# The last six of nine token blocks of a second feed-forward layer: plain blocks replaced by Strassen pairs

## Chip, cores and metric

The kernel runs on one core of a Trainium2 chip. The metric is the device time of one execution in microseconds (us); lower is better. Engines are named as in the profile: PE is TensorE's matmul side and PEld its weight load, DVE is VectorE, ACT is ScalarE, POOL is GpSimd, SP is SyncE, which here only issues DMAs.

## What is computed

A chunked attention is followed by two feed-forward layers over 4608 tokens with model width 512 and hidden width 2048. Only the second layer is touched by the change.

```python
def _moe2_ref(x, w_in, w_out, s, b):      # x 4608x512, w_in 512x2048, w_out 2048x512
    h = x @ w_in
    r = np.maximum(h, 0.0)
    g = s * (r * r) + b
    return (g @ w_out).astype(np.float32)
```

## The kernel before

The 4608 tokens are cut into `NB` = 9 blocks of `TB` = 512. A layer is 9 x 16 = 144 steps, one for each block and each of the `MF` = 16 tiles of 128 hidden columns; steps 0 to 143 are the first layer and 144 to 287 the second. Activations and weights are kept as two parts, hi and lo (`xh`, `xl`, and the pairs of `w_in` and `w_out`), and a product is three matmuls: hi by hi, hi by lo, lo by hi. So a step has 24 matmuls, each with a 128x128 weight tile and 512 columns: `mm1` (L451 to L453) does 4 tiles of the contraction x 3, and `mm2` (L469) does 4 output tiles x 3, two steps behind (`LAG`). All 32 pairs of weight tiles of a layer stay in SBUF (`wp`, tags `w0_0` to `w1_15`).

Between the two, each step of the second layer takes the hidden tile out of PSUM on ACT with Relu, Square and an affine Identity (`ew_a`, L576 to L578), and DVE makes its hi and lo parts (`ew_hi` L614, `ew_lo` L618). The hidden tile has three PSUM banks in turn (`h_bank`), and the output of a block has four (`acc0`, `acc1`), which `evac` empties once in 16 steps. `x2_load` fetches the next block from DRAM scratch (`x2d`), and `store` sends rows of 512 floats to the output. The first two blocks of a layer are run in two halves, since their weights are still being prepared.

Every engine runs its instructions in the order in which they stand. Up to step 33 that order is a table (`START`), from 128 to 165 another (`TURN`); elsewhere it is the loop over `i`, and from step 166 on that loop does the rest of the second layer. SP issues nearly all DMAs, in order, and no more than eight of them are open at a time: each waits for the landing of the one that had its semaphore before. `mm2_last` does the last two steps of `mm2` output tile by output tile, with a store after each.

## Time and profile before

| | |
|---|---|
| device time, median of 3 runs | 1712.54 us (1711.9 to 1712.77) |
| span of the profiled execution, first to last instruction | 1710.9 us |
| PE busy | 1662.3 us, 97% |
| DVE busy | 1026.4 us, 60% |
| ACT busy | 979.8 us, 57% |
| POOL busy | 675.2 us, 39% |
| DMA traffic | 100.24 MB, mean 59 GB/s |

The page gives the span and not the execution's own device time; the median of the runs is 1.6 us above the span. Busy shares are means over stages that differ: in the last third of the span, where the second layer's plain steps run, DVE and ACT are far less busy than in the first two. A matmul's record is longer than the pace at which matmuls follow each other, since they are pipelined, so the pace is read from how many start in a stretch.

### The profile page before, as it was taken

How to read it: one execution, taken by the hardware profiler on the slowest of the kernel's cores; microseconds unless marked ns; L12 is line 12 of the kernel's file. 1: busy time of each engine (PE TensorE's matmuls, PEld its weight loads, DVE VectorE, ACT ScalarE, POOL GpSimd, SP SyncE). 2: the span in 40 equal slices, each digit the busy share in tenths (PEclk: the TensorE clock that was granted, in tenths of full speed). 3: DMA queues.
4: the chain of work that ended last, by engine and by line, in shares of the span. 5: the costliest groups of instructions: out<-in, count | busy, mean ns of one | idle time of the engine just before them, and what ended most of it. 6: DMA issues, size and time to landing. Idle time of an engine off the chain costs nothing.

```text
span 1710.9 us, 25404 instructions
## 1 busy us (share of the span) xinstructions
PE 1662.3 (97%) x9424; PEld 1365.1 (80%) x9424; DVE 1026.4 (60%) x1652; ACT 979.8 (57%) x1590; POOL 675.2 (39%) x576
## 2 busy tenths in 40 slices
PE   4789999999999999999999999999999999999998
PEld 3568777888888888888888888888888888888887
DVE  5899998887887878887799675322222222222222
ACT  5877765666666666666777776443444443434433
POOL 4678865655655656666667553000000000000000
PEclk8799999999999999999999999999999999999999
DMA  9634224222122222121312342101010000101010
GB/s 216 152 109 116 75 58 98 38 59 35 31 58 38 63 35 55 33 60 32 124 52 97 117 151 86 37 16 30 21 25 25 22 28 15 36 8 43 0 25 25
DMA packets 220859, 100.24 MB, mean 59 GB/s; under 512 B 182336, under 2 KB 198720, under 8 KB 220736
## 3 DMA queue, kind: packets, MB, share of 16 engines
q1 hardware_dynamic: 215344, 94.69, 22.0%
q10 hardware_dynamic: 5392, 3.93, 0.9%
q8 instruction: 74, 1.21, 0.3%
q14 instruction: 49, 0.40, 0.1%
HBM read 75.50 MB, written 23.07 MB: 58 GB/s over the span
## 4 chain that ended last, share of the span: by engine, by line
PE 89%; DVE 5%; ACT 2%; DMA 2%; issue 1%; SPq 1%; POOL 1%; ACTq 0%; DVEq 0%; POOLq 0%
PE acc L469 42%; PE h L451 15%; PE h L453 14%; PE h L452 14%; PE pat L343 1%; PE pat L318 1%; PE pat L282 1%; DMA wst<-in_moe_w_in_dram 1%; DVE h L603 1%; DVE t L604 1%; DVE ah L602 1%; DVE w L396 0%; DVE t L585 0%; POOL w L399 0%; DMA vs<-in_v_dram 0%
## 5 line engine op out<-in xcount | busy, mean ns | idle before, releaser
L451 PE MATMUL h<-xh,w 128*128 128x512 f32 x1152 | 457.0, 397 | 10.2 <-DVE t L604 6.2
L453 PE MATMUL h<-xh,w 128*128 128x512 f32 x1152 | 450.0, 391 | 0.0
L452 PE MATMUL h<-xl,w 128*128 128x512 f32 x1152 | 449.7, 390 | 0.0
L576 ACT ACTIVATE r<-h 128x512 f32<-128x512 f32 x144 | 85.9, 596 | 382.4 <-PE h L453 372.1
L469 PE MATMUL acc<-gh,w 128*128 128x512 f32 x1152 | 285.5, 390 | 0.6 <-ACT gh L612 0.6
L469 PE MATMUL acc<-w,gh 128*128 128x512 f32 x1136 | 280.5, 389 | 0.0
L614 DVE CAST gh<-r 128x512 fp32r<-128x512 f32 x134 | 60.9, 455 | 339.3 <-ACT r L578 326.6
L451 PEld LDWEIGHTS h<-xh,w 128*128 128x128 f32 x1152 | 216.9, 188 | 59.0 <-DVE t L604 8.3
L453 PEld LDWEIGHTS h<-xh,w 128*128 128x128 f32 x1152 | 216.9, 188 | 46.3
L469 PEld LDWEIGHTS acc<-gh,w 128*128 128x128 f32 x1152 | 215.6, 188 | 46.0 <-ACT gh L612 1.0
L452 PEld LDWEIGHTS h<-xl,w 128*128 128x128 f32 x1152 | 217.2, 189 | 43.9 <-DVE xl L359 0.5
L469 PEld LDWEIGHTS acc<-w,gh 128*128 128x128 f32 x1136 | 213.2, 188 | 44.3
L564 POOL TENSOR_SCALAR r<-ah,ab_sb 128x512 f32<-128x512 f32 x138 | 111.0, 805 | 234.3 <-ACT ah L547 234.1
L567 POOL TENSOR_TENSOR r<-r,ah 128x512 f32<-128x512 f32 x140 | 182.7, 1305 | 13.7 <-ACT r L562 2.2
L618 POOL TENSOR_TENSOR gl<-t,gh 128x512 fp32r<-128x512 f32 x129 | 168.1, 1304 | 16.1 <-ACT gh L612 14.2
L469 PE MATMUL acc<-gl,w 128*128 128x512 f32 x576 | 154.1, 389 | 0.0
L469 PE MATMUL acc<-w,gl 128*128 128x512 f32 x568 | 151.8, 389 | 0.0
L602 DVE SCALAR_TENSOR_TENSOR ah<-r,h 128x512 f32<-128x512 f32 x144 | 98.3, 682 | 78.5 <-ACT h L595 78.5
L612 ACT ACTIVATE gh<-t 128x512 fp32r<-128x512 f32 x144 | 90.9, 631 | 77.0 <-DVE t L604 71.0
L469 PEld LDWEIGHTS acc<-gl,w 128*128 128x128 f32 x576 | 108.0, 188 | 22.6 <-POOL gl L618 0.3
L399 POOL TENSOR_TENSOR w<-w,wst 128x512 int32<-128x512 int32 x64 | 93.9, 1477 | 78.0 <-DVE w L396 47.8
L469 PEld LDWEIGHTS acc<-w,gl 128*128 128x128 f32 x568 | 106.6, 188 | 22.2
(92 smaller groups left out, 2147.4 us busy)
## 6 DMA issues: line engine op xcount, KB each, us to landing
wst<-in_moe_w_out_dram SPq DMA_DIRECT2D x30, 512.0 KB, 4.6
wst<-in_moe_w_in_dram SPq DMA_DIRECT2D x29, 512.0 KB, 5.0
x2d<-o SPq DMA_DIRECT2D x52, 256.0 KB, 2.7
...
out_dram<-o SPq DMA_DIRECT2D x68, 128.0 KB, 2.4
...
```

The costliest lines, as they stand in the source:

```text
L399: eng.tensor_tensor(out=w, in0=w, in1=st[:, :, 0], op=ALU.add)
L451: T.matmul(h, wh, xh[:, kk], start=kk == 0, stop=False)
L452: T.matmul(h, wh, xl[:, kk], start=False, stop=False)
L453: T.matmul(h, wl, xh[:, kk], start=False, stop=kk == KD - 1)
L469: T.matmul(o, l, r, start=first and n == 0, stop=last and n == 2)
L564: eng.tensor_scalar(out=r, in0=ah, scalar1=ab_sb[:, 1:2], scalar2=ab_sb[:, 0:1], op0=ALU.mult, op1=ALU.add)
L567: eng.tensor_tensor(out=r, in0=r, in1=ah, op=ALU.mult)
L576: A.activation(r, h_t[i], AF.Relu)
L602: V.scalar_tensor_tensor(out=t, in0=r, scalar=ONE, in1=y, op0=ALU.add, op1=ALU.mult)
L612: A.activation(gh, tmp[i]["g"], AF.Copy)
L614: V.tensor_copy(gh, tmp[i]["g"])
L618: (eng or (G if i < N1 else V)).tensor_tensor(out=gl, in0=tmp.pop(i)["g"], in1=f(g_t[i][0]), op=ALU.subtract)
```

## The change

The program is the same, instruction by instruction, up to the start of step 166 on every engine. From there a new function, `finish`, replaces the loop. Steps 166 to 191, which end the two halved blocks and block 2, stay plain. The remaining six blocks become three pairs, and each pair of blocks is multiplied by Strassen's scheme in the variant with 15 sums, in both matmuls of the layer: 7 products of quarter size in place of 8.

- **Weights.** During the plain steps `conv` runs 16 times. Each run joins hi and lo of two weight tiles (`whole`), makes four sums (`tt`), splits them again (`hi` on ACT, `lo` on DVE), and writes the seven operands to DRAM scratch `wq_d` (`as_is`, `put`). In the pairs, `wi_load` and `wo_load` bring them back, 512 KB a time, 84 and 84 in all.
- **Input of a pair.** `x_load` fetches its two blocks from `x2d`; DVE makes four sums of 128x1024 (`x_part`), ACT and DVE split seven operands (`x_hi`, `x_lo`).
- **First matmul of a pair.** It has 8 sets of 7 products (`m1`), each of 6 matmuls. Four hidden tiles of a set come from three chains of PSUM banks: `chain` copies a partial sum out of bank A on ACT before PE goes on adding to it, and `h_sum` adds the other bank's part on DVE.
- **Between.** `g_relu` and `g_square` on ACT, four sums (`mix`) on DVE, and seven splits (`g_hi` on ACT, `g_lo` on DVE). Scale and bias move behind the second matmul: the column sums of `w_out` (`csum_add` on POOL, `bias_mm`) give the bias.
- **Second matmul.** It has 14 half products (`m2`) for every two sets, each of 6 matmuls, so 56 a pair. Each is added into `acc` in SBUF (`out_add`, 48 a pair on DVE and 8 on ACT); eight `out_affine` on ACT bring the bias in.
- **Output.** It comes out transposed; `leave` turns it in 32x32 squares on DVE and `leave_out` writes it with 64 DMAs a pair, each of 32 KB in runs of 32 floats. In the last pair, ACT issues half of them.
- **Order.** `Plan` lists all these steps with costs, dependencies and counts of free tiles, and sorts them by a greedy list schedule (`order`). PE's own order is fixed by hand: in the pairs one product of the first matmul alternates with one half product of the second, 14 places behind; the last 14 half products of the last pair stand alone. `m1_op` and `m2_op` hold what each waits for.

```diff
-X2 = (41,) + tuple(range(52, 140, 16))
+ORDER = (1, 2, 6, 5, 7, 4, 3)
...
+    wq_d = {(k, u): dram.tile([P, 14, 2, 2 * P], F32, name=f"wq{k}_{u}") for k in range(2) for u in range(HF // 2)}
...
-    def mm2_last():
...
+        def add(self, name, eng, cost, fn, *args, after=(), take=None, give=(), lat=0.1, early=None, two=False, kb=0):
...
+            now = {n: max(0.0, o["due"] - o["early"]) if o["early"] is not None else 0.0 for n, o in ops.items()}
...
+                    key = (s, o["due"])
+                    if best is None or e == best[3] and (s < best[0] - 0.05 or abs(s - best[0]) <= 0.05 and o["due"] < best[1]) or e != best[3] and key < best[:2]:
+                        best = (s, o["due"], n, e)
...
+    def finish():
+        i0, i1 = TURNED, N1 + 3 * MF
+        plan = Plan()
+        op = plan.add
+        MM = 0.2267
+        PRE = i1 - 5
...
+            def whole(x):
+                if x == 0:
+                    load()
+                h = f(w_tiles[kind, s + HF * x])
+                V.tensor_tensor(out=st["w"][:, x], in0=h[:, 0], in1=h[:, 1], op=ALU.add)
+
+            def as_is(k, x, y):
+                SP.dma_start(out=at(k), in_=f(w_tiles[kind, s + HF * x])[:, :, y * 2 * P:(y + 1) * 2 * P])
...
+            def tt(o, i, j, how):
+                V.tensor_tensor(out=cut(*o), in0=cut(*i), in1=cut(*j), op=how)
...
+            def hi(x):
+                st[x] = spare.tile([P, 2, 2, 2 * P], F32R, "wo")
+                A.activation(st[x][0][:, :, 0], st["w"][:, x].rearrange("p (n c) -> p n c", n=2), AF.Copy)
+
+            def lo(x, eng):
+                o = st[x][0]
+                eng.tensor_tensor(out=o[:, :, 1], in0=st["w"][:, x].rearrange("p (n c) -> p n c", n=2), in1=f(o[:, :, 0]), op=ALU.subtract)
+
+            def put(x, ks):
+                for y, k in enumerate(ks):
+                    SP.dma_start(out=at(k), in_=f(st[x][0][:, y]))
...
+            op(p + "s1", "V", 0.44, tt, a22, a21, a22, ALU.add, after=[p + "w1"], two=True)
+            op(p + "s3", "V", 0.44, tt, a21, a11, a21, ALU.subtract, after=[p + "s1"], two=True)
+            op(p + "s2", "V", 0.44, tt, a11, a22, a11, ALU.subtract, after=[p + "s3"], two=True)
+            op(p + "s4", "V", 0.44, tt, a12, a12, a11, ALU.subtract, after=[p + "s2"], two=True)
+            if kind:
+                op(p + "cs", "G", 1.4, csum_add, after=[p + "s4"])
...
+        def bias_mm():
+            o = ps["bias"] = ps_a.tile([P, TB], F32, tag="att", name="pb")
+            for z in range(KD):
+                for x in (0, 2) if z < 2 else (0,):
+                    T.matmul(o[:, z:z + 1], csum[:, (z + x) * P:(z + x + 1) * P], ones, start=x == 0, stop=x == 2 or z >= 2)
...
+        def x_load(t):
...
+            xx[t] = {0: r0[:, 0:2], 1: r0[:, 2:4], 3: r1[:, 0:2], 5: r0[:, 2:4], 6: r1[:, 2:4]}
+            for y in range(2):
+                SP.dma_start(out=hold["raw"][y], in_=x2d[PAIRS[t][y]].rearrange("k p c -> p k c"))
...
+        def x_part(t, what):
+            r0, r1 = hold["raw"]
+            b11, b21, b12, b22 = r0[:, 0:2], r0[:, 2:4], r1[:, 0:2], r1[:, 2:4]
+            if what == "T3":
+                xx[t][4], xx[t, 4] = main.tile([P, 2, N], F32, "t3")
+                V.tensor_tensor(out=xx[t][4], in0=b22, in1=b12, op=ALU.subtract)
+            elif what == "T1":
+                V.tensor_tensor(out=b12, in0=b12, in1=b11, op=ALU.subtract)
+            elif what == "T2":
+                xx[t][2], xx[t, 2] = main.tile([P, 2, N], F32, "t2")
+                V.tensor_tensor(out=xx[t][2], in0=xx[t][4], in1=b11, op=ALU.add)
+            else:
+                V.tensor_tensor(out=b21, in0=b21, in1=xx[t][2], op=ALU.subtract)
...
+        def x_hi(t, k):
+            xs[t, k] = main.tile([P, 2, N], F32R, "xs"), main.tile([P, 2, N], F32R, "xs")
+            A.activation(xs[t, k][0][0], xx[t][k], AF.Copy)
+
+        def x_lo(t, k, eng):
+            (hi, _), (lo, _) = xs[t, k]
+            eng.tensor_tensor(out=lo, in0=xx[t][k], in1=f(hi), op=ALU.subtract)
...
+        def wo_load(y):
+            wo[y] = main.tile([P, 2, 2, 2 * P], F32R, "wo2")
+            u, z = divmod(y % (7 * NG), 7)
+            SP.dma_start(out=f(wo[y][0]), in_=wq_d[1, u][:, 2 * z:2 * z + 2])
...
+        def m1(t, s, k):
+            p = ORDER[k]
+            b = "C" if p == 2 else "E" if p in (5, 3) else "A"
...
+            q = 7 * (NSETS * t + s) + k
+            w, tag = wi[q // 2]
+            w = w[:, q % 2]
+            (hi, _), (lo, _) = xs[t, k]
+            terms = [(z, 0, hi) for z in range(2)] + [(z, 1, hi) for z in range(2)] + [(z, 0, lo) for z in range(2)]
+            for n, (z, l, x) in enumerate(terms):
+                T.matmul(ps[b], w[:, l, z * P:(z + 1) * P], x[:, z], start=n == 0 and p in (1, 2, 5), stop=n == 5, skip_group_check=True)
...
+        def chain(t, s, c):
+            A.activation(g_new(t, s, c), ps["A"], AF.Copy)
+
+        def h_sum(t, s, c):
+            g = gt[t, s, c]
+            V.tensor_tensor(out=g, in0=ps["C" if c == "11" else "E"], in1=g, op=ALU.add)
+
+        def g_relu(t, s, c):
+            if c == "21":
+                A.activation(g_new(t, s, c), ps["A"], AF.Relu)
+            else:
+                A.activation(gt[t, s, c], gt[t, s, c], AF.Relu)
...
+        def g_square(t, s, c):
+            A.activation(gt[t, s, c], gt[t, s, c], AF.Square)
...
+        def mix(t, s, c):
+            o, i, j, how = {
+                "22": ("22", "22", "12", ALU.subtract), "12": ("12", "12", "11", ALU.subtract),
+                "11": ("11", "22", "11", ALU.add), "21": ("21", "21", "11", ALU.subtract),
+            }[c]
+            V.tensor_tensor(out=gt[t, s, o], in0=gt[t, s, i], in1=gt[t, s, j], op=how)
...
+        def g_hi(t, s, c, k):
+            gx[t, s, k] = main.tile([P, 2, N], F32R, "gs")
+            A.activation(gx[t, s, k][0][:, 0], gt[t, s, c], AF.Copy)
+
+        def g_lo(t, s, c, k):
+            g = gx[t, s, k][0]
+            V.tensor_tensor(out=g[:, 1], in0=gt[t, s, c], in1=f(g[:, 0]), op=ALU.subtract)
...
+        def m2(t, u, j):
...
+            if p == 2:
+                pool, tag = (ps_a, "att") if dp else (ps_h, "h2")
+                ps["c2", dp] = pool.tile([P, TB], F32, tag=tag, name="hc2")
...
+            for n, (e, l, g) in enumerate(terms):
+                T.matmul(
+                    o, w[:, e, l, dp * P:(dp + 1) * P], gx[t, 2 * u + e, k][0][:, g],
+                    start=n == 0 and p in (1, 2, 5), stop=n == 5, skip_group_check=True,
+                )
+            if dp:
...
+        def out_add(t, u, k, dp):
+            if "acc" not in hold:
+                hold["acc"] = [xp.tile([P, KD, N], F32, tag=tag, name="acc") for tag in ("xh", "xl")]
+            y, z = where[ORDER[k]]
+            o, i = hold["acc"][y][:, z + dp], bank2(k, dp)
+            if u == 0 and ORDER[k] in (1, 6, 5, 4):
+                A.activation(o, i, AF.Copy)
+            elif u == NG - 1:
+                V.scalar_tensor_tensor(out=o, in0=i, scalar=s_sb, in1=o, op0=ALU.mult, op1=ALU.add)
+            else:
+                V.tensor_tensor(out=o, in0=i, in1=o, op=ALU.add)
...
+        def leave(t, y, z):
+            lt[t, y, z] = small.tile([P, N], F32, "ot")
+            V.transpose(lt[t, y, z][0], hold["acc"][y][:, z])
+
+        def leave_out(t, y, z, h, both):
+            o, tag = lt[t, y, z]
+            s0 = PAIRS[t][y] * CH
+            rows = out.rearrange("(b s) d -> s b d", b=B)
+            for x in range(4):
+                (A if both else SP).dma_start(
+                    out=rows[s0 + 32 * h:s0 + 32 * h + 32, :, z * P + 32 * x:z * P + 32 * x + 32],
+                    in_=o[32 * x:32 * x + 32].rearrange("p (b h i) -> p b h i", b=B, h=2)[:, :, h],
+                )
...
+            b4 = f"{t},{s - 1}" if s else f"{t - 1},{NSETS - 1}"
+            c = f"{t},{s}"
+            wait = {
+                0: [f"r21{b4}"] if t or s else [f"Kr{PRE - 1}", f"Kr{PRE - 2}", f"Kr{PRE - 3}"], 1: [f"hs11{b4}", "biasout" if s or t else None], 2: [f"c11{c}"], 3: [f"hs12{b4}"],
+                4: [f"c12{c}"], 5: [f"c22{c}"], 6: [f"hs22{c}"],
+            }[k]
...
+            if last and k in (1, 4, 5, 6):
+                op(f"lv{t},{y},{z}", "V", 0.72, leave, t, y, z, after=[f"o{k}{c},{dp}"], take=("s", 1))
+                for h in range(2):
+                    act = h == 1 and t == NPR - 1
+                    op(f"lo{t},{y},{z},{h}", "A" if act else "S", 2.4, leave_out, t, y, z, h, act, after=[f"lv{t},{y},{z}", f"lo{t},{y},{z},0" if h else None], lat=2.5, kb=128, give=[("s", 1)] if h else ())
...
+                op(f"wi{q // 2}", "S", 0.55, wi_load, q // 2, after=[made[0, s_, k_] for s_, k_ in kk], take=("m", 1), lat=2.5, kb=512, early=AHEAD)
...
+        AHEAD, HOLD = 9.0, 16.0
+        for i in range(i0, i1):
...
+        for z in range(14 - slot):
+            l1(slot)
+            slot += 1
+        for z in range(len(every)):
+            if slot < len(every):
+                l1(slot)
+                slot += 1
+            l2(z)
+        order = plan.order({"m": 0, "s": 4, "c": 6})
+        for n in order:
+            o = plan.ops[n]
+            o["fn"](*o["args"])
+        return plan
 
     with tc.manual_schedule():
...
-            for j, at in enumerate(X2, 2):
-                if e == at:
-                    x2_load(j)
-                if 2 <= e - at < 2 + KD:
-                    x2_hi(j, e - at - 2)
-                    x2_lo(j, e - at - 2)
-        mm2_last()
+            if i % N1 in (3 * HF - 1, 4 * HF - 1):
+                part_load(steps[i][0])
+
+        wq.extend(due(1))
```

**In the plain steps and inside a pair**, PE's row of work looked like this (`acc`: output banks; `h`: hidden bank; `w_0` to `w_15`: weight tiles):

```order
L469 MATMUL acc_14133<-w_13_10844,gh 128x512 x2
L469 MATMUL acc_14134<-w_13_10844,gh 128x512 x2
L469 MATMUL acc_14133<-w_13_10844,gl 128x512 x2
L469 MATMUL acc_14134<-w_13_10844,gl 128x512 x2
L451 MATMUL h<-xh,w_0_9142 128x512
L452 MATMUL h<-xl,w_0_9142 128x512
L453 MATMUL h<-xh,w_0_9142 128x512
```

and now, inside the first pair (`ae`, `hc_`: output banks; `hA`, `hc`, `hE`: hidden banks; `wi`, `wo`: loaded weight operands), it is:

```order
L1033 MATMUL ae_12395<-gs,wo_12282 128x512 x6
L972 MATMUL hc<-xs,wi 128x512 x6
L1033 MATMUL ae_12396<-gs,wo_12282 128x512 x6
L972 MATMUL hA<-xs,wi 128x512 x6
L1033 MATMUL hc_12448<-gs,wo_12334 128x512 x6
L972 MATMUL hE<-xs,wi 128x512 x6
L1033 MATMUL hc_12478<-gs,wo_12334 128x512 x6
```

Twelve matmuls of one kind in a row have become six, and every six go to a bank whose earlier content another engine has to take first. On ACT, at the same place, before (`r`: hidden tile):

```order
L576 ACTIVATE r_14883<-h_14870 128x512
L577 ACTIVATE r_14883<-r_14883 128x512
L578 ACTIVATE r_14883<-r_14883,b2_sb_95,s_sb_94 128x512
L576 ACTIVATE r_14916<-h_14903 128x512
L577 ACTIVATE r_14916<-r_14916 128x512
L578 ACTIVATE r_14916<-r_14916,b2_sb_95,s_sb_94 128x512
```

and now (`g11` to `g22`: the four hidden tiles of a set; `gs`: operands of the second matmul):

```order
L983 ACTIVATE g12_12767<-hA_12701 128x512
L996 ACTIVATE g11_12717<-g11_12717 128x512
L1007 ACTIVATE gs_12792<-g21_12528 128x512
L1007 ACTIVATE gs_12794<-g21_12671 128x512
L983 ACTIVATE g22_12810<-hA_12701 128x512
L993 ACTIVATE g22_12810<-g22_12810 128x512
L996 ACTIVATE g22_12810<-g22_12810 128x512
```

Two copies out of bank `hA_12701` stand four places apart; PE may add to the bank again only behind each of them, with one half product of the second matmul between the second copy's source and its next use.

**Where one pair passes to the next**, SP had, before (`o`: output tiles):

```order
L487 DMA out_0_dram<-o_13540 64x512 x4
L487 DMA out_0_dram<-o_13543 64x512 x4
L424 DMA xl_13656<-x2d7_88 128x512 x4
L487 DMA out_0_dram<-o_14098 64x512 x4
L487 DMA out_0_dram<-o_14101 64x512 x4
L424 DMA xl_14214<-x2d8_89 128x512 x4
L487 DMA out_0_dram<-o_14656 64x512 x4
L487 DMA out_0_dram<-o_14659 64x512 x4
```

and now (`ot`: turned output tiles; `wi`, `wo2`: weight operands):

```order
L1071 DMA out_0_dram<-ot_13563 32x8x32 x4
L949 DMA wi_13592<-wq0_1_91 128x1024
L954 DMA wo2_13602<-wq1_0_94 128x1024
L1071 DMA out_0_dram<-ot_13600 32x8x32 x4
L1071 DMA out_0_dram<-ot_13563 32x8x32 x4
L949 DMA wi_13654<-wq0_1_91 128x1024
L954 DMA wo2_13658<-wq1_0_94 128x1024
L1071 DMA out_0_dram<-ot_13600 32x8x32 x4
L1071 DMA out_0_dram<-ot_13639 32x8x32 x4
L949 DMA wi_13711<-wq0_1_91 128x1024
L954 DMA wo2_13723<-wq1_0_94 128x1024
```

Eight stores of 32 KB now stand between one pair of weight loads and the next. DVE, at the same place, had before:

```order
L618 TENSOR_TENSOR gl_14642<-r_14603,gh_14640 128x512
L525 COPY o_14659<-acc1_14134 128x512 x2
L614 CAST gh_14679<-r_14636 128x512
L618 TENSOR_TENSOR gl_14681<-r_14636,gh_14679 128x512
L614 CAST gh_14722<-r_14675 128x512
```

and now:

```order
L1011 TENSOR_TENSOR gs_13519<-g11_13356,gs_13519 128x512
L1052 SCALAR_TENSOR_TENSOR acc_12420<-ae0_12395,s_sb_102,acc_12420 128x512
L1052 SCALAR_TENSOR_TENSOR acc_12419<-hc2_13395,s_sb_102,acc_12419 128x512
L1064 STREAM_TRANSPOSE ot_13563<-acc_12419 128x512
L1011 TENSOR_TENSOR gs_13555<-g11_13517,gs_13555 128x512
L1052 SCALAR_TENSOR_TENSOR acc_12420<-ae1_12396,s_sb_102,acc_12420 128x512
L1011 TENSOR_TENSOR gs_13567<-g21_13471,gs_13567 128x512
L1011 TENSOR_TENSOR gs_13582<-g22_13447,gs_13582 128x512
L1064 STREAM_TRANSPOSE ot_13600<-acc_12419 128x512
L1052 SCALAR_TENSOR_TENSOR acc_12419<-ae0_12395,s_sb_102,acc_12419 128x512
```

Output additions (L1052), turns (L1064) and splits (L1011) share DVE's row.

## Rows read from the trace of the kernel before

**Rows 1.** The page: span, busy time by engine, and the span in 40 slices.
```profile
span 1710.9 us, 25404 instructions
...
PE 1662.3 (97%) x9424; PEld 1365.1 (80%) x9424; DVE 1026.4 (60%) x1652; ACT 979.8 (57%) x1590; POOL 675.2 (39%) x576
...
PE   4789999999999999999999999999999999999998
...
PEclk8799999999999999999999999999999999999999
```

**Rows 2.** Windows: busy us (x instructions) of PE, PEld, DVE, ACT, POOL, clock, DMA.
```profile
1041.50:1705.50 664.00, 664.00 (x2931) 549.55 (x2929) 172.83 (x299) 274.44 (x414) 9.01 (x7) 1.00 0.10 26
```

**Rows 3.** Waits from 1100 to 1650 us: total, times, longest.
```profile
ACT r L576 <- PE h L453: 314.9, 101, 3.3
```

**Rows 4.** Timeline at 1300 us: start, duration, engine, line.
```profile
1300.01 0.39 PE L453 MATMUL h<-xh,w 128*128 128x512 f32 x1
...
1300.44 0.60 ACT L576 ACTIVATE r<-h 128x512 f32<-128x512 f32 x1 [3.33 <-PE h L453]
...
1303.10 0.69 DVE L432 TENSOR_TENSOR xl<-xl,xh 128x512 fp32r<-128x512 f32 x1 [4.69 <-ACT xh L428]
...
1303.71 0.42 DVE L614 CAST gh<-r 128x512 fp32r<-128x512 f32 x1
```

**Rows 5.** Groups by shape, DVE and ACT, 1100 to 1650 us: total, mean ns.
```profile
L618 DVE TENSOR_TENSOR gl<-r,gh 128x512 fp32r<-128x512 f32 x101 | 70.9, 702 | 13.5 <-PE acc L469 2.7 <-DVE gh L614 0.5
...
L578 ACT ACTIVATE r<-r,b_sb,s_sb 128x512 f32<-128x512 f32 x102 | 83.2, 816 | 3.4
L577 ACT ACTIVATE r<-r 128x512 f32<-128x512 f32 x102 | 64.5, 632 | 3.3
L576 ACT ACTIVATE r<-h 128x512 f32<-128x512 f32 x101 | 60.4, 598 | 314.9 <-PE h L453 314.9
```

**Rows 6.** The same over the whole span: DVE, ACT, PE.
```profile
L586 DVE SCALAR_TENSOR_TENSOR t<-t,a_sb,h 128x512 f32<-128x512 f32 x144 | 107.7, 748 | 5.1
...
L585 DVE TENSOR_TENSOR t<-t,h 128x512 f32<-128x512 f32 x144 | 97.0, 673 | 9.6 <-ACT ah L547 4.7 <-ACT t L553 3.4
...
L270 DVE STREAM_TRANSPOSE qkT<-qk 128x512 f32<-128x512 f32 x56 | 36.4, 687 | 0.1
...
L523 ACT ACTIVATE o<-acc 128x1024 f32<-128x1024 f32 x10 | 10.2, 1022 | 0.4 <-PE acc L469 0.3
...
L259 PE MATMUL pat<-ident,qk 128*128 128x128 f32 x52 | 12.0, 399 | 18.3 <-DMA qk<-in_q_dram 11.7 <-issue 3.9 <-ACT eT L328 2.4
```

**Rows 7.** Timeline of SP's issues: start, duration, line, count.
```profile
301.51 3.79 SPq L216 DMA_DIRECT2D qk<-in_q_dram  x8
305.35 4.75 SPq L216 DMA_DIRECT2D qk<-in_k_dram  x8
...
981.76 0.50 SPq L376 DMA_DIRECT2D wst<-in_moe_w_out_dram  x1
```

**Rows 8.** The page, DMA issues: count, KB each, us to landing.
```profile
wst<-in_moe_w_out_dram SPq DMA_DIRECT2D x30, 512.0 KB, 4.6
...
out_dram<-o SPq DMA_DIRECT2D x68, 128.0 KB, 2.4
```

**Rows 9.** Windows: the last two numbers are DMA share and GB/s.
```profile
301.00:307.00 6.00, 6.00 (x86) 4.85 (x85) 5.83 (x11) 2.77 (x6) 3.47 (x4) 1.00 0.32 50
307.00:313.00 6.00, 6.00 (x28) 4.95 (x28) 4.66 (x10) 4.52 (x8) 3.29 (x4) 1.00 0.36 63
...
980.00:990.00 10.00, 10.00 (x46) 8.29 (x45) 4.11 (x5) 8.47 (x14) 4.41 (x4) 1.00 0.88 301
```

**Rows 10.** Timeline at the end of the span.
```profile
1705.38 0.40 PE L499 MATMUL acc<-w,gl 128*128 128x512 f32 x1
...
1706.55 0.42 DVE L503 COPY o<-acc 128x256 f32<-128x256 f32 x1 [0.99 <-ACT o L502]
1707.00 0.50 ACTq L487 DMA_DIRECT2D out_dram<-o  x1
```

More of the change, by code (lines that the diff above doesn't have):

```diff
@@ L236, in tile_chunk_attention__then__rational_ffn__then__relu2_ffn, with big @@
     turn = itertools.count()
+    bigs = itertools.cycle(range(4))
+    def big(shape, dtype, name):
+        return ap_.tile(shape, dtype, tag=f"big{next(bigs)}", name=name, bufs=1)
     begun = -1
@@ L447, in mm1 @@
         ph = 0 if jj < NB else 1
-        h = h_bank(i)
+        h = h_bank(i) if bank is None else bank
         for kk in range(KD):
@@ L751, in tile_chunk_attention__then__rational_ffn__then__relu2_ffn @@
         play(START)
[L753 to L760 removed]
+        for i in range(BEGUN, TURN_AT):
+            mm1(i)
             att_out(2 * i - 1, 0)
```

437 lines of the change are left out of this document (396 added, 41 removed).

## Prediction

> **What bounds the kernel now.** I read the page first, then a window over the stretch that the change replaces, then who waits for whom in it. The page has PE busy for 97% of 1710.9 us, with all slices but the first three and the last at 9 and a clock granted in full from the third on [rows 1]. From 1041.5 to 1705.5 us, which is step 166 to the end, PE is busy for 664.00 of 664.00 us, and 2931 matmuls start [rows 2]; the program has 122 steps x 24 = 2928 there. One matmul therefore takes 664.00 / 2931 = 0.2265 us, and a plain step 5.44 us. ACT waits for PE 101 times, 314.9 us in all [rows 3], while no wait of PE in this stretch shows: PE is the bound. What takes matmuls off PE shortens the span, as long as the others keep up with the new pattern. The question is what they do then.
>
> **What is removed.** A pair has 2 x 16 steps x 24 = 768 matmuls now, and 8 x 7 x 6 + 56 x 6 = 672 afterwards. Three pairs save 288 x 0.2265 = **65.2 us**. A pair then takes 152.2 us of PE, and one of its eight sets 19.03 us. Of the work added there PE itself has only `bias_mm`: six matmuls of one column and a wait for column sums. The nearest row is a 128x128 transpose of 0.399 us [rows 6], so 6 x 0.4 = 2.4 us at most if nothing waits, and I take **2 us** (0 to 4).
>
> **DVE in the pairs.** Per set: 3 `h_sum` with an operand in PSUM at 0.673 [rows 6], 4 `mix` and 7 `g_lo` at 0.702 [rows 5], 9.74 us. Per pair: 48 `out_add`, 34 at 0.673 and 14 with a scale at 0.748 [rows 6], 33.4 us; 11 of 128x1024, taken as two of 0.702, 15.4 us; 8 turns at 0.687 [rows 6], 5.5 us. Together 8 x 9.74 + 54.3 = 132.2 us of 152.2, 87%. It is not even. By the order, between one `h_sum` of tile 11 and the next, DVE has 18.5, 18.5, 19.1 and 19.1 us in the four sets around the passage from pair to pair, against 19.03 us of PE. Durations overstate DVE: an operation of 0.69 us started at 1303.10 and the next, independent one at 1303.71, 0.61 later [rows 4]. With 25 operations a set that gives back up to 2 us. So DVE keeps pace but has nothing to spare in eight sets. I charge these 0 to 1.5 us each and take 0.4, **3 us**.
>
> **ACT in the pairs.** Per set 4 reads of PSUM at 0.598 and 14 operations at 0.632 [rows 5], 11.2 us; per pair 8 more reads, 8 affine at 0.816 [rows 5] and 7 of 128x1024 at 1.022 [rows 6], 18.5 us. Sum 108.4 of 152.2 us, 71%. The load is not the danger, the latency is. The second copy out of bank A (`c22`) must be over before the next-but-one group of PE, and only one half product lies between, 6 x 0.2265 = 1.36 us. The row: the last matmul of a step starts at 1300.01, ACT at 1300.44 [rows 4], that is 0.2 us after PE's slot of 0.23 is over; then 0.60 us of copy and about 0.1 back. 0.9 of 1.36 us, so 0.4 us are left, less than one ACT operation. If ACT has just begun a split (0.63) PE waits some 0.2 us. 24 sets at 0 to 0.5 us; I take 0.12, **3 us**.
>
> **Loads of weights.** 168 loads of 512 KB in 24 sets are 3.67 MB per 19.03 us, 193 GB/s. The trace has 301 GB/s at a share of 0.88 for 10 us [rows 9], so 342 at full share, and the loads want 56%. A load lands after some 4.6 us [rows 8], and the planner may start it 9 us ahead of its due time; away from a passage they cost nothing. If this cover fails, PE stands.
>
> **The passage from pair to pair.** Here lie the 64 stores of 32 KB. In the first passage SP has 64 stores and 18 loads in a row, which feed 36 groups of PE, 36 x 1.36 = 48.9 us. The nearest row to such a store is the load of q and k, with the same 32x8x32 shape: 8 in 3.79 us and the next 8 in 4.75 [rows 7], 0.54 us each from start to start; a load of weights takes 0.50 [rows 7]. 64 x 0.54 + 18 x 0.50 = 43.6 us. SP is nearly full but not over. The DMA engines: in 12 us, 20 issues of such short runs took a share of 0.32 and 0.36 [rows 9], 4.1 us of all engines, 0.2 each; 64 make 13 us, 18 loads at 342 GB/s 27.6, sum 41 of 48.9 us. Every weight load stands behind eight stores, so what a store takes more than this falls on PE. Two passages at 0 to 12 us; I take 2 each, **4 us**, since both sums stay under 48.9.
>
> No row of before shows a write to DRAM in runs under 512 bytes. The Trainium skill, DMA: Bandwidth & Descriptors, section Specifications, says that below 512 B a DMA engine does a read-modify-write. No run here shows it; by that rule a store here would cost more than the q load that I took, and the time would be that of the second rival below, some 1689 us in place of 1667.
>
> **Plain steps 166 to 191.** 26 x 5.44 = 141 us. Sixteen `conv` bring DVE 16 x (4 x 0.70 + 4 x about 0.40) = 70 us beside some 45 of its own and the first input; 7 DMAs of 256 KB each make 1.8 MB per 8 us. Both fit. I take **1 us** (0 to 4).
>
> **The end.** Now the last matmul is over at 1705.78 and the span at 1710.9, 5.1 us with half a copy, an issue of 0.50 and a store [rows 10]. Afterwards the last 14 half products run alone, at 1.36 us each, and each goes to a bank that DVE must empty one group earlier: 0.2 + 0.75 us and a turn in between are close to 1.36, **1.5 us** (0 to 4). Six outputs are turned in the last six groups. SP has 24 stores for them, and ACT 24 more beside it. The first is ready 5 x 1.36 before PE's end plus 0.2 + 0.75 + 0.69, 5.2 us before; 24 x 0.54 = 13.0 us bring SP to 7.8 us after PE's end, and a store lands 2.4 us later [rows 8]: 10.2, which is **5 us** more than now (3 at 0.47 an issue; 9 where stores land late).
>
> **Sum.** 65.2 - 2 - 3 - 3 - 4 - 1 - 1.5 - 5 = 45.7 us. The span would be 1665.2 us. The page does not give the execution's own time, and the median of the runs is 1.6 us above the span, so I forecast 1666.8, **1667 us**. With every cost at its low end (3 us for the end alone) it would be 1650; with those of this case at their middle to upper ends 1677.
>
> **Rivals.**
> 1. *Nothing waits.* Bias 1, end 3, nothing else: 1712.5 - 61 = 1652 us. For it: DVE's overlap [rows 4] and its low charge per operation. Against it: nine tenths of DVE and of SP in the same 50 us.
> 2. *The stores hold up the loads.* If a short write takes twice the engines' time of the short read, a passage needs 26 + 27.6 = 54 us of 48.9; if it lands so late that eight open DMAs bind, say 6 us, an issue takes 0.75 and the passage 82 x 0.75 = 61.5. That is 5 to 12.6 us a passage in place of 2, and 24 x 0.75 instead of 13 at the end, 5 more, with late landing up to 8: 1667 + 6 to 21 + 5 to 8, about 1689 us. For it: no row shows such a write. Against it: 0.2 us for the read.
> 3. *In-order rows feed each other's lateness.* DVE late by 1.5 us in the eight full sets and ACT's copy by 0.5 in all 24 make 12 + 12 in place of 6: 1685 us. For it: 0.4 us of slack behind `c22`. Against it: the overlap.
> 4. *The weight stream is the bound (slower).* Weights that lay in SBUF now come from DRAM, 88.1 MB in 3 x 152.2 = 456.7 us. The saving is gone when this takes 457 + 46 us, at 175 GB/s. At 144 GB/s it is 612 us and the kernel takes 1667 + 155 = 1822 us. Against it: 301 GB/s over 10 us, though on reads of another shape [rows 9].
>
> **Chances.** Forecast 0.55, rival 1 0.08, rival 2 0.20, rival 3 0.14, rival 4 0.03. The range leaves out rival 4, the better half of rival 1 and the worse half of rival 2: 1653 to 1694 us. 0.2% (3.4 us) is about what can be told from no change; all cases but rival 4 are faster by far more. Faster 0.96, same 0.01, slower 0.03.
>
> **What would show it.** In the profile afterwards PE starts 288 - 6 matmuls fewer, and inside a pair a window of 19 us has 84 of them at full clock. Idle time ahead of `m1` and `m2` should be under 1 us a set, put down to ACT (bank A) and DVE. At the passages SP's row should show stores about 0.54 us apart; a PE that waits for `wi` or `wo2` there speaks for rival 2, idle time spread over all sets for rival 3, and waits for weights away from the passages for rival 4. DVE near 87% and ACT near 71% inside a pair test the counts. The forecast is wrong if the end takes over 14 us or a passage over 4.

## The result and the profile after

The changed kernel takes 1671.19 us (median of four, 1670.4 to 1672.47) against 1712.46 us before: ratio 0.976, 95% interval 0.9747 to 0.9774. The forecast was 1667.0, its range 1653 to 1694. The profiled execution took 1671.37 us for a span of 1669.6, so the span fell by 41.3 us [rows 1], where 65.2 us of matmuls left PE. Where the other 23.9 us went is the question of what follows.

The page of the changed kernel, busy time, and two lines of the 40 slices:

```profile
PE 1607.8 (96%) x9148; PEld 1315.7 (79%) x9148; DVE 1310.4 (78%) x2063; ACT 1092.1 (65%) x1824; POOL 690.1 (41%) x584
...
PE   4799999999999999999999999899999999999997
...
PEclk8899999999999999999999999899999999999999
```

PE starts 276 matmuls fewer: 288 less, and 12 rows for the six of the bias. Before, every slice between the third and the last was at 9 [rows 1]; now one slice in the twenties is not, in PE and in its clock: the 26th, some 1044 to 1085 us. That is the stretch of plain steps with the weight sums beside them, not the pairs. The windows say the same (PE busy and matmuls, granted clock, DMA share, GB/s; a window counts every matmul that overlaps it). The first line is of the kernel before, the others of the changed one:

```profile
1041.50:1080.00 38.50, 38.50 (x172) 1.00 0.29 83
...
1041.50:1080.00 38.50, 32.29 (x122) 0.87 0.88 290
...
1065.00:1070.00 5.00, 0.93 (x3) 0.85 1.03 364
1070.00:1075.00 5.00, 5.00 (x12) 0.50 1.00 349
```

The first window holds 122 matmuls where it held 172; at 0.2265 us each that is some 11 us lost. A busy PE is not a working PE: from 1070 to 1075 us it is busy all the time with 12 matmuls, where 5 us at full clock start 22, since its clock was granted at 0.50, the level of 1.2 GHz, after 4 us of waiting. All waits of PE from 1041 us to the end (total, times, longest):

```profile
PE acc L478 <- DVE o L523: 4.1, 1, 4.1
PE acc L478 <- ACT gh L610: 2.1, 1, 2.1
PE ae L1033 <- DVE acc L1054: 1.2, 2, 0.6
PE ae L1033 <- DVE acc L1052: 0.7, 1, 0.7
PE hA L972 <- ACT g L983: 0.7, 1, 0.7
PE ae L1033 <- ACT gs L1007: 0.3, 1, 0.3
```

No weight load is among them. The first two are the plain steps, and the timeline of the four engines shows how each came about (start, duration, engine, line, count, and the idle time before with what ended it):

```profile
1045.41 0.63 ACT L413 ACTIVATE w<-w 128x512 fp32r<-128x512 f32 x1 [4.66 <-POOL w L406]
1045.94 0.61 ACT L610 ACTIVATE gh<-r 128x512 fp32r<-128x512 f32 x1
...
1046.61 2.57 PE L478 MATMUL acc<-w,gh 128*128 128x512 f32 x8 [2.08 <-ACT gh L610]
...
1062.70 5.76 DVE L441 TENSOR_TENSOR xl<-xl,xh 128x512 fp32r<-128x512 f32 x4
1068.39 1.27 DVE L523 COPY o<-acc 128x512 f32<-128x512 f32 x2
...
1064.45 3.46 POOL L530 TENSOR_TENSOR o<-o 128x512 f32<-128x512 f32 x2 [0.50 <-ACT o L521]
...
1069.72 2.93 PE L478 MATMUL acc<-w,gh 128*128 128x512 f32 x6 [4.07 <-DVE o L523]
```

First hole: the rounding of step 165's hidden tile (L610) went from DVE to ACT, where it stands behind the last weight's rounding (L413), which waits 4.66 us for POOL. Second hole: the eviction of the first half's sums (`evac`, L523) stands on DVE behind four `x2_lo` (L441), which take 1.44 us each and not 0.7, while POOL adds beside them; PE has nowhere to put the next block's sums. PE's restart is slow as well: six matmuls in 2.93 us, where full clock takes 1.5.

The passage from pair to pair and the end:

```profile
1387.87 5.63 SPq L1071 DMA_DIRECT2D out_dram<-ot  x8
...
1648.45 11.21 PE L1033 MATMUL ae<-gs,wo 128*128 128x512 f32 x48 [0.70 <-DVE acc L1052]
...
1649.04 17.51 SPq L1071 DMA_DIRECT2D out_dram<-ot  x32
```

SP has stores and loads in one row from 1358 to 1406 us, and PE waits for none of them. The last matmul is over at 1659.7, the span 9.9 us later.

### The profile page after: what moved, and what is told of

Same layout as the page of the kernel before. It is cut to its first block, busy times and chain, and to the rows that moved or that the text cites. A ratio compares the mean times of both kernels' runs of the same rounds, so it can differ in the third digit from the quotient of the medians.

```text
span 1669.6 us, 26182 instructions
## 1 busy us (share of the span) xinstructions
PE 1607.8 (96%) x9148; PEld 1315.7 (79%) x9148; DVE 1310.4 (78%) x2063; ACT 1092.1 (65%) x1824; POOL 690.1 (41%) x584
## 4 chain that ended last, share of the span: by engine, by line
PE 83%; DVE 10%; issue 2%; ACT 2%; POOL 2%; DMA 1%; SPq 0%; DVEq 0%; ACTq 0%; POOLq 0%
PE acc L478 26%; PE ae L1033 12%; PE h L460 9%; PE h L462 9%; PE h L461 9%; PE hA L972 8%; PE hE L972 4%; PE hc L972 2%; PE hc L1033 2%; PE pat L350 1%; DVE h L601 1%; PE pat L325 1%; PE pat L289 1%; DVE t L602 1%; DVE ah L600 1%
## 5 line engine op out<-in xcount | busy, mean ns | idle before, releaser
L460 PE MATMUL h<-xh,w 128*128 128x512 f32 x768 | 308.4, 402 | 9.0 <-DVE t L602 5.0
L461 PE MATMUL h<-xl,w 128*128 128x512 f32 x768 | 301.4, 392 | 0.3 <-DVE xl L366 0.3
L462 PE MATMUL h<-xh,w 128*128 128x512 f32 x768 | 301.3, 392 | 0.0
L1033 PE MATMUL ae<-gs,wo 128*128 128x512 f32 x864 | 219.6, 391 | 2.3 <-DVE acc L1054 1.2
L1033 PEld LDWEIGHTS ae<-gs,wo 128*128 128x128 f32 x864 | 161.7, 188 | 38.8 <-DVE acc L1054 2.4
L460 PEld LDWEIGHTS h<-xh,w 128*128 128x128 f32 x768 | 145.5, 189 | 43.1 <-DVE t L602 8.3
L616 POOL TENSOR_TENSOR gl<-t,gh 128x512 fp32r<-128x512 f32 x129 | 167.7, 1301 | 16.1 <-ACT gh L610 14.4
L462 PEld LDWEIGHTS h<-xh,w 128*128 128x128 f32 x768 | 145.5, 189 | 31.5
L461 PEld LDWEIGHTS h<-xl,w 128*128 128x128 f32 x768 | 145.6, 190 | 29.2 <-DVE xl L366 0.6
L972 PE MATMUL hA<-xs,wi 128*128 128x512 f32 x576 | 146.7, 390 | 0.7 <-ACT g L983 0.7
L610 ACT ACTIVATE gh<-t 128x512 fp32r<-128x512 f32 x144 | 90.9, 631 | 78.3 <-DVE t L602 70.5
L972 PEld LDWEIGHTS hA<-xs,wi 128*128 128x128 f32 x576 | 108.0, 188 | 23.9 <-ACT g L983 1.1
L593 ACT ACTIVATE h<-ah,exb 128x512 f32<-128x512 f32 x144 | 99.5, 691 | 38.5 <-DVE t L584 35.9
L588 ACT ACTIVATE ah<-r,lnb 128x512 f32<-128x512 f32 x144 | 103.4, 718 | 30.1 <-POOL r L565 29.7
```

The source lines that it names most:

```text
L460: T.matmul(h, wh, xh[:, kk], start=kk == 0, stop=False)
L461: T.matmul(h, wh, xl[:, kk], start=False, stop=False)
L462: T.matmul(h, wl, xh[:, kk], start=False, stop=kk == KD - 1)
L588: A.activation(tmp[i]["ah"], tmp[i]["r"], AF.Ln, scale=RS, bias=lnb)
L593: A.activation(h_t[i], tmp[i]["ah"], AF.Exp, scale=-1.0, bias=exb)
L616: (eng or (G if i < N1 else V)).tensor_tensor(out=gl, in0=tmp.pop(i)["g"], in1=f(g_t[i][0]), op=ALU.subtract)
```

## The experiments

**A fixed order.** The planner picks among equals in the iteration order of a set of names, so each build comes out a little different, and the rows of the order ahead of the prediction are of one such build. For edits that move nothing else, all kernels but the two compared above have the order written out as this trace shows it. In its names `M` and `R` are the two matmuls of a plain step, `Kr`, `Ks`, `Ka`, `H` and `y` its Relu, Square, Identity, rounding and `lo` part, `ev` and `ew` the halves of an eviction on ACT and on DVE, `xh` and `xl` the split of block 2's input, and `c` with a number a run of `conv`; in the pairs `P` and `Q` are the products of the two matmuls and `o` the additions `out_add`.

```diff
-        order = plan.order({"m": 0, "s": 4, "c": 6})
+        order = (
+            'M166 H165 pl167 c0w0 y165 c0w1 c2w0 c0as1 R164 Kr166 c0s1 ...
...
+        ).split()
```

> The changed kernel with the order of its list-scheduled part written out as the trace of the changed kernel shows it, engine by engine, in place of the planner (which breaks ties between equal operations by the iteration order of a set of names, so that it gives another order at each build). It is the base of the three edits beside it. Both theories expect the time of the changed kernel again, 1671 us within 1.5, with the two holes of TensorE: 2.1 us of wait at 1046 us and 4.1 us at 1069 us.

1670.72 us, the same as the changed kernel, with the same waits of 4.1 and 2.1 us. It is the base of what follows; a difference under some 1.5 us between two kernels tells nothing. The kernel before, run beside each group of kernels, took 1712.2 to 1713.4 us.

**The first hole alone.**

```diff
-            op(f"H{i}", "A", 0.64, ew_hi, i, True, after=[f"Ka{i}", f"R{i - 2}"])
+            op(f"H{i}", "A", 0.64, ew_hi, i, i >= i0, after=[f"Ka{i}", f"R{i - 2}"])
...
+        order.remove(f"H{i0 - 1}")
+        order.insert(0, f"H{i0 - 1}")
```

> The fixed order, with the rounding (ew_hi) of the last hidden tile ahead of the list-scheduled part on VectorE, where it stood before, in place of ScalarE, where it stands behind the rounding of the last weight, which waits 4.7 us for GpSimd's addition. Theory A (place in the queue): the hole at 1046 us closes, and with it the stretch at half clock behind it; 4 us less than the fixed order, 1667. Rival B (the weights: the last tiles of the second layer are rounded too late in any case, and TensorE would wait for them at the same place): 0 to 1 us less. Rival C (the plain stretch is limited by transfers, whose share is 0.76 to 0.99 of the engines there): what is won here is lost at the next hole, 0.

1670.6 us: 0. The hole at 1046 us did close, but PE's timeline has a new wait in its place:

```profile
1065.86 1.22 PE L478 MATMUL acc<-w,gh 128*128 128x512 f32 x2 [4.46 <-ACT o L521]
1070.64 2.93 PE L478 MATMUL acc<-w,gh 128*128 128x512 f32 x6 [3.56 <-DVE o L523]
```

PE reached the eviction 4 us earlier, and the eviction was no earlier. Rival C was right as to the number.

**The second hole alone.**

```diff
+        late = [f"xl{kk}" for kk in range(KD)]
+        order = [n for n in order if n not in late]
+        at = order.index(f"y{N1 + 3 * HF + 2}") + 1
+        order[at:at] = late
```

> The fixed order, with the four subtractions x2_lo of the third plain block moved on VectorE from ahead of the eviction of the first block's sums to behind the split of step 170; nothing else moves. Theory A (place in the queue): the hole at 1069 us, in which TensorE waits 4.1 us for that eviction, closes with the half-clock stretch behind it, 7 us less than the fixed order, 1664. Rival B (VectorE is late for another reason: it waits for its weight sums' tiles, which wait for stores): the eviction starts with the accumulation's end all the same but TensorE then waits for the split of the next step, 3 us or less is won. Rival C (transfers limit the stretch): 0.

1665.01 us, 5.7 less than the base: theory A. The four `x2_lo` (shortest, median, longest in ns) in the base, beside POOL's additions, and here, where they stand alone:

```profile
L441 DVE TENSOR_TENSOR xl<-xl,xh x4: 679/1756/1798, 1062.6 to 1066.6; 128x512 fp32r<-128x512 f32 x4
```

```profile
L441 DVE TENSOR_TENSOR xl<-xl,xh x4: 681/683/683, 1070.1 to 1071.9; 128x512 fp32r<-128x512 f32 x4
```

**Both.** The two edits together.

> Both edits, of the first split and of the eviction. Theory A: the two holes are independent, 11 us less than the fixed order, 1660, and the plain stretch to 1080 us takes some 27 us as 120 matmuls at full clock should. Rival C (transfers limit the stretch): 0 to 3 us less in all, and a new wait for a transfer or for a tile that a store holds shows before 1080 us.

1665.26 us, no more than the second edit alone; the 11 us of theory A did not come. The rows of ACT, DVE and PE show what is late now:

```profile
1062.40 0.69 DVE L824 TENSOR_TENSOR wf<-w 128x512 f32<-128x512 f32 x1 [2.41 <-DMA wq<-wo]
...
1064.39 0.63 ACT L840 ACTIVATE wo<-wf 128x512 fp32r<-128x512 f32 x1 [1.19 <-DVE wf L833]
...
1065.97 1.06 ACT L521 ACTIVATE o<-acc 128x512 f32<-128x512 f32 x2
...
1067.08 3.42 PE L478 MATMUL acc<-w,gh 128*128 128x512 f32 x8 [4.30 <-ACT o L521]
```

A weight sum on DVE (L824) waits 2.41 us until a store has left its tile; a rounding on ACT (L840) waits for that sum; the eviction (L521) stands behind the rounding; PE waits for the eviction. The planner's model gives such a store of 256 KB 256 / 330 + 2.5 = 3.3 us until it has landed; in this trace, at a DMA share near 1, it is 5.3 (median from 1040 to 1070 us).

**Evictions ahead of the weight sums.** The first edit, and this part of the order:

```diff
-R167 Kr169 xl2 c4as1 c3hi1 xl0 Ks169 c4as0 c3cs c3hi0 c5as0 M170 ew167 ev167 ...
+R167 Kr169 ev167 ew167 c4as1 Ks169 c4as0 c3cs M170 Ka169 ae167 H169 R168 c3hi1 c3hi0 ...
```

> e3 gained nothing over e2 because a wait of 4.3 us for ScalarE's half of the same eviction took the place of the hole that was closed: on ScalarE it stands behind two roundings of weight sums, which wait for VectorE's sums, and these wait 2.4 us for a tile that a store to DRAM still holds. This kernel is e3 with both halves of the eviction and the split of step 168 put ahead of everything that waits for a transfer: on ScalarE the eviction comes right behind the ReLU of step 169, then the rest of that step, then the weight sums' roundings and the roundings of the third block's input; on VectorE the split of step 168 and the eviction come ahead of the next weight sum. Theory A (in-order queues carry the lateness of the stores into the eviction): no hole before 1080 us, 11 us less than the fixed order, 1660. Rival C (transfers limit the stretch itself): the hole moves to the next tile that a store holds, 1663 to 1665 as e2 and e3.

1668.49 us (1665.39 to 1669.69; the trace is of the fastest of these runs), no better than e3. The window up to 1080 us is now nearly as it was before the change, 169 matmuls against 172, but the lateness comes out at the next eviction (ACT, then PE):

```profile
1041.50:1080.00 38.50, 38.47 (x169) 1.00 0.90 296
...
1106.12 0.63 ACT L840 ACTIVATE wo<-wf 128x512 fp32r<-128x512 f32 x1 [3.84 <-DVE wf L833]
...
1107.36 1.06 ACT L521 ACTIVATE o<-acc 128x512 f32<-128x512 f32 x2
...
1108.47 3.43 PE L478 MATMUL acc<-w,gh 128*128 128x512 f32 x8 [3.54 <-ACT o L521]
```

**The second eviction too.**

```diff
-R175 c4s2 Kr177 free01 c8s2 Ks177 c4s4 c8s4 c4hi0 c9s4 c13as0 Ka177 c4lo0 c14as0 M178 ev175 ew175 ...
+R175 Kr177 ev175 ew175 Ks177 Ka177 H177 free01 c13as0 c14as0 M178 ad175 c13as1 c13as5 R176 ...
```

> e4 closed both holes before 1080 us (169 matmuls between 1041.5 and 1080 us) but one of 3.5 us and half clock behind it opened at 1105 us: the eviction of the second block on ScalarE stood behind a rounding of a weight sum, which waited for VectorE, which had waited 3.0 us for a tile that a store held. This kernel is e4 with the second eviction, too, put right behind the ReLU of step 177, and the weight sums of that stretch behind the split of step 177. Theory A (the same mechanism, once for each eviction): the hole at 1105 us closes, 1660 to 1662. Rival C (what is won is given back at whatever waits next for a transfer, so the stretch ends at the same time): 1665 to 1669 as e4.

1664.06 us, 6.7 less than the base, but 2 to 4 short of theory A, and only 1 less than the second edit alone, less than can be told apart. Two waits stay, of 1.8 us at 1103 and of 1.0 at 1108 us. The first (DVE and PE):

```profile
1101.21 1.29 DVE L824 TENSOR_TENSOR wf<-w 128x512 f32<-128x512 f32 x2 [3.01 <-DMA wq<-wo]
...
1103.16 1.20 PE L478 MATMUL acc<-w,gl 128*128 128x512 f32 x4 [1.79 <-DVE gl L616]
```

A step's split (L616), and for the second wait DVE's half of the eviction (L523), stand there behind weight sums in the same way. So the mechanism is shown, work that waits for transfers queued ahead of work that PE waits for, and not one place of it: the hole of the base closes with 5.7 us won (e2), the one at 1105 us with 4.4 (e8 against e4), while e1, e3 and e4 let the wait appear further on. Transfers by themselves do not stop PE: in e4 it ran from 1041.5 to 1080 us at full clock beside a DMA share of 0.90. Whether some order wins back all of the 11 us is not shown: some 4 are still lost in e8's plain steps, and there rival C is not ruled out.

**The waits in the pairs.**

```diff
-... f120,7 Q0,3,4 c221,0 wi33 o60,2,0 f120,6 hs221,0 P1,0,5 af0,1,0 wo26 o60,2,1 ...
+... f120,7 o60,2,0 o60,2,1 Q0,3,4 c221,0 wi33 f120,6 hs221,0 P1,0,5 af0,1,0 wo26 ...
```

The second pair has the same move, of `o61,2,0` and `o61,2,1`.

> e8 with, in the first and second pair, the two additions out_add of the third group's product with the short name 6 moved on VectorE ahead of the matmul that they waited for: they read one half of an accumulator tile whose other half that matmul (the fifth of the fourth group) writes, and stand behind it in the program though they do not need its result; the trace shows VectorE idle for 2.06 us until that matmul's end at 1344.05 us, and then TensorE waiting 0.6 us for the second of them. Theory F (a false order through the shared tile, not a full row of VectorE): the two waits of 0.6 us at 1346 and 1500 us are gone, 2 us less than e8. Rival A (VectorE's row too full): the waits stay or move, 0.

1661.61 us, 2.5 less than e8; the two waits for L1054 are gone. In the base they looked so (PE, and DVE between):

```profile
1342.53 1.52 PE L1033 MATMUL ae<-gs,wo 128*128 128x512 f32 x6
...
1344.09 0.69 DVE L1054 TENSOR_TENSOR acc<-ae,acc 128x512 f32<-128x512 f32 x1 [2.06 <-PE ae L1033]
...
1346.03 1.66 PE L1033 MATMUL ae<-gs,wo 128*128 128x512 f32 x6 [0.62 <-DVE acc L1054]
```

DVE did not lack time: it stood idle for 2.06 us until a group of matmuls that writes the other half of the tile it reads was over (1342.53 + 6 x 0.2265 = 1343.9). Theory F. This is the fastest kernel, 0.9697 of before (0.9683 to 0.971).

**DVE's load.** The same question from the other side.

```diff
-            return op(f"xl{t},{k}", eng, 1.36 if eng == "V" else 2.7, x_lo, t, k, V if eng == "V" else G,
+            return op(f"xl{t},{k}", eng, 1.36 if eng == "V" else 2.7, x_lo, t, k, G if t else V,
```

> The fixed order, with the 14 subtractions x_lo (128x1024) of the second and third pair on GpSimd in place of VectorE. Theory A (VectorE's row is too full ahead of a passage; the two waits of 0.6 us at 1346 and 1500 us come from that): 1 to 3 us less. Rival E (an operation of VectorE takes 1.76 us in place of 0.68 beside an addition of GpSimd, as x2_lo did in the fixed order, so the row gets fuller, and the two waits are a matter of the order in the row): 5 to 20 us slower, with VectorE's operations at twice their length and new waits of TensorE for VectorE from 1300 to 1360 and from 1460 to 1520 us.

1672.05 us, the base within 1.5: neither theory as told. The waits of 0.6 us stay, so a full row was not their cause, but nothing got slower either. DVE's groups from 1300 to 1350 us, in the base and here (count, total, mean ns):

```profile
L1011 DVE TENSOR_TENSOR gs<-g,gs 128x512 fp32r<-128x512 f32 x16 | 10.4, 683 | 0.1
L927 DVE TENSOR_TENSOR t<-raw 128x1024 f32<-128x1024 f32 x1 | 1.2, 1216 | 0.0
```

```profile
L1011 DVE TENSOR_TENSOR gs<-g,gs 128x512 fp32r<-128x512 f32 x18 | 15.7, 912 | 0.0
L1054 DVE TENSOR_TENSOR acc<-ae,acc 128x512 f32<-128x512 f32 x11 | 7.6, 689 | 5.3 <-PE ae L1033 5.2
L927 DVE TENSOR_TENSOR t<-raw 128x1024 f32<-128x1024 f32 x1 | 3.1, 3149 | 0.0
```

Beside GpSimd, DVE's operations on SBUF alone got longer, those with an operand in PSUM (L1054, 689 ns against 686 in the base) did not. What the move freed went into that: from 1200 to 1640 us DVE is busy for 327.8 us, against 328.8 in the base.

**Stores and weights.** How near are the rivals that did not come about?

```diff
-            for x in range(4):
+            for x in (0, 1, 2, 3) * (1 if t else 2):
                 (A if both else SP).dma_start(
```

> The fixed order, with each of the 64 short stores of the first pair issued twice on SyncE's queue (the same bytes to the same place). Theory A (the passage between two pairs is free as long as SyncE's row keeps up; in the fixed order SyncE issues without a pause from 1358 to 1408 us and TensorE waits for no weight tile, so little room is left): 64 more issues of 0.55 us are 35 us, less the 5 to 10 us that the loads run ahead: 25 to 30 us slower, 1698, TensorE waiting for weight tiles between 1370 and 1440 us. Rival B (the DMA engines set it, whose share is 0.78 to 1.03 there): the same sign, but the issues themselves get longer than 0.55 us and the share stays at 1. Rival C (there is room): within 3 us of the fixed order.

1710.34 us, 39.6 slower, more than the 25 to 30 expected. SP, its waits for landed stores from 1355 to 1440 us (total, times, longest), PE, and a window with all engines left out but PE:

```profile
1359.47 3.79 SPq L1071 DMA_DIRECT2D out_dram<-ot  x8
...
1388.20 10.19 SPq L1071 DMA_DIRECT2D out_dram<-ot  x16
...
SPq L1071 <- DMA out_dram<-ot: 19.7, 8, 3.9
...
1391.25 2.90 PE L972 MATMUL hE<-xs,wi 128*128 128x512 f32 x6 [3.82 <-DMA wi<-wq]
...
1380.00:1400.00 20.00, 15.94 (x57) 0.83 0.51 103
```

Eight stores that nothing holds take 3.79 us, 0.47 each. Sixteen in a row take 10.19, because SP stands in between: the second copy of a store goes to the same place as the first and waits until that has landed, with two loads of weights ahead of it. (The fifth of these 16 starts at 1392.65 us, 4.45 after the first.) SP's row is the limit, as theory A has it, with the DMA engines half idle. But 64 x 0.47 = 30 us of it are stores, and the 19.7 us of waits belong to the way in which this edit doubles them, so it overstates what 64 other stores would cost. PE's waits for loads are 23.7 us; the rest is that each longer wait is followed by matmuls at half clock (six in 2.90 us). In that window 27 stores of 32 KB and 1.2 MB of loads take 10.2 us of all engines; at 342 GB/s the loads are 3.4, so a store costs some 0.25 us of the engines.

```diff
+            for _ in range(2):
+                SP.dma_start(out=f(wi[y][0]), in_=wq_d[0, u][:, 2 * z:2 * z + 2])
```

> The fixed order, with each of the 84 loads of the first matrix's weight sums (512 KB) issued twice. Theory A (the weight stream has room: DMA share 0.67 over 1200 to 1640 us, and the 44 MB more are 0.24 of it at the 400 GB/s of the busiest slices): 0 to 6 us slower, the most of it in the passages, where the share is near 1 already. Rival D (the stream is the bound, or nearly): 30 us or more slower, TensorE waiting for weight tiles all through the pairs.

1809.86 us, but it doesn't measure what it was made for: SP's waits (total, times, longest) show that the second copy waits for the first's landing in the same tile, with everything queued behind it.

```profile
SPq L950 <- DMA wi<-wq: 370.2, 78, 10.4
```

```diff
             SP.dma_start(out=f(wi[y][0]), in_=wq_d[0, u][:, 2 * z:2 * z + 2])
+            G.dma_start(out=extra_d[y % 4], in_=f(wi[y][0]))
```

> e6 did not measure the weight stream: the second copy of a load goes into the tile of the first, waits on SyncE's queue until that has landed (370 us of waits), and holds up all that is queued behind it. This kernel is the fixed order with the same 44 MB more, but beside SyncE's queue: as soon as a tile of the first matrix's weight sums has landed, GpSimd, which does nothing in the pairs, issues a copy of it to a scratch place in DRAM, 84 copies of 512 KB. Theory A (the stream has room: share 0.67 at 217 GB/s over 1200 to 1640 us, and 44 MB in 560 us are 79 GB/s more, 0.24): 0 to 6 us slower, most of it in the passages. Rival D (the stream is the bound, or nearly): 30 us or more slower, with waits of TensorE for weight tiles all through the pairs.

1671.07 us, nothing. The window that had a share of 0.72 and 244 GB/s in the base, and the loads' time to landing from 1200 to 1640 us:

```profile
1200.00:1340.00 140.00, 139.31 (x613) 1.00 0.94 343
...
wi<-wq SPq DMA_DIRECT2D x77, 512.0 KB, 6.8
```

44 MB more, loads that land after 6.8 us and not 4.2, and no wait of PE for a weight: rival D is out.

**The end.**

```diff
-                (A if both else SP).dma_start(
+                (G if t == NPR - 1 and x == 3 else A if both else SP).dma_start(
```

> e9 with every fourth short store of the last pair issued on GpSimd's queue, so that SyncE and ScalarE issue 24 each and GpSimd 16. Theory A (the end is the issuing of 64 short stores by two queues at 0.55 us each, 17.5 us from 1649 us on, and what is left of it when the last matmul is over): the last issue is 4 us earlier, but the last tile is ready only 2 us after the last matmul, so 2 to 3 us less than e9. Rival G (GpSimd's issues take twice as long or more, or the landing sets the end): 0, or slower.

1664.92 us, 3.3 slower than e9: rival G. GpSimd's issues (shortest, median, longest in ns) are not long, but the last seven start from 1654.2 to 1660.3 us, 1 us apart, later than SP's and ACT's last (1657.6 and 1658.7), and the span ends behind them. The two windows are of e9 and of this kernel (PE, clock, DMA share, GB/s):

```profile
L1071 POOL DMA_DIRECT2D out_dram<-ot x16: 582/584/755, 1641.9 to 1660.3; - x16
...
1648.00:1657.00 9.00, 2.78 (x13) 0.84 0.88 128
...
1648.00:1657.00 9.00, 4.25 (x19) 0.99 0.98 128
```

Two queues already kept the DMA engines at a share of 0.88, and the third moved nothing more: 128 GB/s both times. The stores land later, 2.2 us (SP) and 2.5 us (ACT, GpSimd) after their issue and not 1.7 to 1.8, and SP and ACT, with eight stores less each, wait for landings in turn. From PE's last matmul to the end of the span it is 11.7 us, 9.9 in e9; the rest of the 3.3 us lies ahead of it and stays open.

## Why the prediction was right, point by point

The time was 4.2 us above the forecast and well inside the range. Against its terms, in us of span:

| term | forecast | measured | from |
|---|---|---|---|
| saving on PE | 65.2 | 65.2 | 276 fewer, bias apart |
| bias | 2 | 1.3 | the 12 rows, 1.39 us in the trace |
| DVE in the pairs | 3 | 1.8 | two waits of 0.6, 0.9 each with the restart |
| ACT behind its copy | 3 | 1.0 | one wait of 0.7 |
| passages | 4 | 0 | no wait for a load |
| plain steps 166 to 191 | 1 (0 to 4) | 11 | x122 against 172 |
| last group | 1.5 | 2 | waits of 0.3 and 0.7, and their gaps |
| end | 5 | 4.8 | 9.9 against 5.1 |

The measured costs come to 21.9 of 23.9 us. The other 2 show as pace and not as a wait (before and after, in a stretch where PE waits for nothing):

```profile
1220.00:1340.00 120.00, 120.00 (x531) 1.00 0.07 18
...
1220.00:1340.00 120.00, 120.00 (x529) 1.00 0.69 239
```

Two matmuls in 531 are 1.7 us over the 457 us of the pairs. What slows them is not shown. That the sum came so near is in part luck: five terms were too high by 8.1 us together, and that hid most of the 10 us by which one was too low.

One row of the kernel before bears on the point on the plain steps below, a DVE operation with two operands in SBUF, first beside an addition of POOL (L399, 1043.52 to 1044.90 us) and then alone:

```profile
1043.83 1.62 DVE L618 TENSOR_TENSOR gl<-r,gh 128x512 fp32r<-128x512 f32 x1
...
1048.13 0.69 DVE L618 TENSOR_TENSOR gl<-r,gh 128x512 fp32r<-128x512 f32 x1
```

- **What bounds the kernel** held: PE is at 9 all through the pairs. The saving, the load on DVE and ACT, and the end (SP's last issue 6.9 us after PE's end, 7.8 in the forecast) were right in kind and size. DVE is busy 89.4 of 120 us inside a pair (1220 to 1340 us), 75% and not 87%, in part since the forecast added durations that overlap [rows 4], and ACT 80.3, 67% and not 71%.
- **The step that was mis-sized is "plain steps", 1 us against 11.** It asked whether DVE's work and the bytes fit into 141 us, and they do. It did not ask what stands in front of what, and it spread the bytes evenly, 1.8 MB per 8 us, where the trace has 290 GB/s from 1041.5 to 1080 us and a share of 1.03 from 1065 to 1070. e2, e4 and e8 show that the loss is a matter of place: weight sums and roundings, which wait for stores, or operations made longer by POOL, ahead of evictions, for which PE waits. The row for the longer DVE operations was not read, though the trace of before has it (1.62 us beside POOL, 0.69 alone, above): the forecast took `x2_lo` and the sums at 0.70 us though POOL adds beside them, and they took up to 1.8. The Trainium skill, SBUF — State Buffer, section "SBUF: two separate sides", says that a DVE operation with two inputs in SBUF and a GpSimd operation that reads SBUF lock each other out for a whole instruction; the traces agree, with 1756 ns against 683 for L441 (base and e2), and with L1054, which reads PSUM and kept its 689 (e7). Half clock after a wait was not counted either: 12 matmuls in place of 22 in 5 us.
- **DVE in the pairs** had the right sum by a wrong reason. Not eight sets that are too tight, but two additions that stand behind a matmul they do not need (e9), with DVE idle before them.
- **Rival 2** failed on its main premise. A short store costs the engines about 0.25 us, not twice the 0.2 of the read, and SP's row took 47.3 us where 43.6 was forecast and 48.9 were there. Its second limb, the eight open DMAs, was at work, though: in the first passage of the base (1355 to 1410 us) SP's stores waited six times, 4.9 us in all, for a load of `wo` to land, and twice, 1.0 us, for one of `wi`. A store that nothing holds was issued faster than the 0.54 us of the forecast (0.47, e5), and that made room for these waits. Little is left: with twice the stores in one passage the saving is all but gone (e5, its own waits among it). The Trainium skill, DMA: Bandwidth & Descriptors, section Specifications, says that below 512 B a DMA engine does a read-modify-write, and the prediction put that at this rival's 1689 us; the traces show no such price, with no wait of PE for a load and 0.25 us a store.
- **Rival 3**, lateness handed on through in-order rows, was put into the pairs; it was at work, but in the plain steps (e3, e4). **Rival 4** is out by e11, **rival 1** by the holes.
